# A hand-ordered attention stage with filler matmuls, row-packet loads and late expert weights

## The chip, the cores and the metric

One core of one Trainium2 chip. The metric is device time in microseconds (us) for one execution, median over runs.

## The reference, cut to what matters

```python
# attention: 8 batches x 8 heads, 576 positions, head size 64
q_p, k_p = phi(q), phi(k)        # relu(x)*cos | relu(x)*sin -> 128 features
kv  = einsum('bhsf,bhsd->bhfd', k_p, v);  z = sum(k_p, axis=2)
out = einsum('bhsf,bhfd->bhsd', q_p, kv) / (q_p . z + 1e-6)
# then 8 experts over 4608 tokens, routed by a balanced (Sinkhorn) table P
for e in range(8):
    out += P[:, e:e+1] * (relu(x @ w1[e]) @ w2[e])
```

## The kernel before: the parts that matter

The attention stage works on 32 head pairs, one after the other in the source; a scheduler orders the instructions on each engine.

```python
ps_num = tile_pool(name="ps_num", bufs=2, space=PSUM)   # also ps_kv 1, ps_tr 3, ps_x 2: 8 banks
for b in range(B):
    for hk in range(NPAIR):
        nc.sync.dma_start(out=q_ld[:, :, 0, :], in_=q_src)      # 256 B rows
        nc.scalar.copy(out=q_ld[:, :, 1, :], in_=q_ld[:, :, 0, :])
        nc.sync.dma_start(out=k_ld, in_=k[...].rearrange("(p c) d -> p c d", c=CH))  # 2304 B; v too
        if b == 0 and hk == 0: w_pre = load_expert_weights(0)
        # VectorE: v_aug (cast), k_p (two passes with cos and sin)
        for hh in range(2):
            # TensorE: nine matmuls of 64 rows into kv_ps[:, hh, :]
            nc.scalar.copy(out=kv_sb[:, hh, :], in_=kv_ps[:, hh, :])
        # TensorE: nine transposes of q into tr_ps; VectorE: ten q_pT
        for hh in range(2):
            # TensorE: five num matmuls; VectorE: five reciprocals (rden)
            # ScalarE: five divisions, st <- num_ps * rden
        # TensorE: five transposes of st into x_ps; VectorE or ScalarE copies x_ps to xT
...
# then logits, Sinkhorn, and 8 experts: 4608 matmuls of 512 columns
```

The softmax here doesn't subtract the row's maximum and nothing guards it: scores larger than these inputs give would overflow.

## Time and profile before

| | before |
|---|---|
| median of 4 runs | 1244.45 us (1244.02 to 1245.35) |
| span of the profiled run | 1240.2 us |
| first expert matmul | 226.3 us |
| time for one head pair, steady | 6.66 us |
| VectorE's own work for a pair | 4.75 us |

The prediction shows the lines that carry this. Two more, from the view of who waited for whom between 60 and 200 us (columns: total us, times, longest us), show the ping-pong of the two engines:

```profile
DVE rden L296 <- PE num_ps L285: 35.6, 40, 1.6
...
PE kv_ps L247 <- DVE k_p L232: 11.1, 20, 1.1
```

VectorE waits for TensorE's num, TensorE for VectorE's k features, and 32 pairs pay for both.

### The profile page before, as it was taken

To read this page: it belongs to the slowest core of one execution; us is meant where nothing else is said; L and a number is where in the kernel's file an instruction comes from. 1 tells how busy PE (TensorE), PEld (TensorE's weight loads), DVE (VectorE), ACT (ScalarE), POOL (GpSimd) and SP (SyncE) were. 2 spreads that over 40 slices of the span, in tenths; PEclk is the share of its full clock that TensorE was granted. 3 is DMA by queue.
4 is the path that set the end of the run, shared out by engine and by line. 5 is a ranking of instruction groups with operands and counts; after the bars stand their busy time and mean duration, and the time that the engine had idled before them with its cause. 6 is when DMAs were issued, how large, how long until landed. Compare 5 with 4: busy or idle time off the path is not lost.

```text
span 1240.2 us, 15100 instructions
## 1 busy us (share of the span) xinstructions
PE 1180.9 (95%) x6032; PEld 577.7 (47%) x6128; DVE 431.5 (35%) x1158; ACT 466.4 (38%) x1051; POOL 1.8 (0%) x10
## 2 busy tenths in 40 slices
PE   4888888899999999999999999999999999999997
PEld 3555555444444444444444444444444444444443
DVE  6776777563132213221322232223222322212221
ACT  4565554531333333333333333333333333333332
POOL 0000000000000000000000000000000000000000
PEclk9655555799999999999999999999999999999999
DMA  9856430300030003000300030003000100001122
GB/s 299 238 127 200 144 115 2 137 1 1 1 128 9 1 1 121 15 1 1 117 20 1 1 115 22 1 1 113 25 1 1 68 1 1 1 1 68 68 80 90
DMA packets 64743, 72.30 MB, mean 58 GB/s; under 512 B 39585, under 2 KB 39585, under 8 KB 64673
## 3 DMA queue, kind: packets, MB, share of 16 engines
q1 hardware_dynamic: 64672, 71.33, 17.7%
q8 instruction: 48, 0.79, 0.3%
q14 instruction: 23, 0.18, 0.0%
HBM read 61.88 MB, written 9.44 MB: 58 GB/s over the span
## 4 chain that ended last, share of the span: by engine, by line
PE 88%; DVE 7%; issue 2%; DMA 1%; ACT 1%; SPq 0%; DVEq 0%; ACTq 0%
PE y_ps L413 40%; PE h_ps L397 39%; PE tr_ps L262 4%; PE kv_ps L247 3%; PE num_ps L285 2%; DVE k_p L232 2%; DVE v_aug L227 1%; DMA wst<-in_moe_w_dram 1%; DVE rden L296 1%; DVE q_pT L270 0%; DVE colp L359 0%; ACT kv_sb L254 0%; PE x_ps L312 0%; ACT st L302 0%; PE lg_ps L333 0%
## 5 line engine op out<-in xcount | busy, mean ns | idle before, releaser
L404 ACT ACTIVATE hT<-h_ps 128x512 bf16<-128x512 f32 x576 | 343.9, 597 | 649.9 <-PE h_ps L397 627.5
L397 PE MATMUL h_ps<-xT,w1e 128*128 128x512 bf16 x2255 | 511.6, 380 | 2.8 <-issue 0.4
L413 PE MATMUL y_ps<-w2e,hT 128*128 128x512 bf16 x2257 | 506.2, 379 | 2.4
L430 DVE SCALAR_TENSOR_TENSOR out_acc<-y_ps,P_tok,out_acc 128x512 f32<-128x512 f32 x252 | 189.2, 751 | 620.3 <-PE y_ps L413 595.7
L413 PEld LDWEIGHTS <-hT 128*128 128x128 bf16 x2304 | 225.4, 98 | 271.0
L397 PEld LDWEIGHTS <-w1e 128*128 128x128 bf16 x2304 | 223.6, 98 | 266.6 <-issue 0.6
L262 PE MATMUL tr_ps<-ident_f,q_ld 128*128 128x128 f32 x288 | 86.9, 431 | 6.7 <-ACT q_ld L213 6.1
L302 ACT ACTIVATE st<-num_ps,rden 128x64 bf16<-128x64 f32 (+1 forms) x320 | 70.5, 314 | 40.1 <-DVE rden L296 37.4
L247 PE MATMUL kv_ps<-v_aug,k_p 64*128 64x65 bf16 x576 | 42.0, 235 | 32.1 <-DVE k_p L232 24.7
L270 DVE SCALAR_TENSOR_TENSOR q_pT<-tr_ps,cs2b 128x128 bf16<-128x128 f32 (+1 forms) x320 | 63.0, 261 | 0.2 <-PE tr_ps L262 0.2
L262 PEld LDWEIGHTS tr_ps<-ident_f,q_ld 128*128 128x128 f32 x288 | 47.2, 210 | 12.2 <-issue 6.0
L247 PEld LDWEIGHTS <-k_p 64*128 64x128 bf16 x576 | 31.5, 122 | 43.1 <-DVE k_p L232 28.9
L422 DVE TENSOR_SCALAR out_acc<-y_ps,P_tok 128x512 f32<-128x512 f32 x36 | 26.9, 750 | 60.0 <-PE y_ps L413 59.9
L285 PE MATMUL num_ps<-kv_sb,q_pT 128*128 128x65 bf16 (+1 forms) x320 | 47.5, 248 | 0.3 <-DVE q_pT L270 0.2
L232 DVE SCALAR_TENSOR_TENSOR k_p<-k_ld,cs 128x576 bf16<-128x576 f32 x64 | 45.2, 742 | 0.9 <-ACT cs L147 0.8
L296 DVE RECIPROCAL rden<-num_ps 128x1 f32<-128x1 f32 (+1 forms) x320 | 27.0, 151 | 51.0 <-PE num_ps L285 49.2
L285 PEld LDWEIGHTS <-q_pT 128*128 128x128 bf16 (+1 forms) x320 | 32.5, 132 | 18.4 <-issue 6.9
L312 PE MATMUL x_ps<-ident_bf,st 128*128 128x128 bf16 (+1 forms) x160 | 33.8, 275 | 5.6 <-ACT st L302 4.2
L254 ACT CAST kv_sb<-kv_ps 128x65 bf16<-128x65 f32 x64 | 13.9, 217 | 51.2 <-PE kv_ps L247 48.8
L108 DVE CAST w1e<-wst 128x2048 bf16<-128x2048 f32 x16 | 19.0, 1222 | 37.4 <-PE h_ps L397 36.9
L312 PEld LDWEIGHTS <-st 128*128 128x128 bf16 (+1 forms) x160 | 16.6, 105 | 29.7 <-ACT st L302 16.9
L213 ACT COPY q_ld<-q_ld 128x576 f32<-128x576 f32 x32 | 21.6, 674 | 9.5 <-DMA q_ld<-in_q_dram 9.4
(41 smaller groups left out, 118.3 us busy)
## 6 DMA issues: line engine op xcount, KB each, us to landing
wst<-in_moe_w_dram SPq DMA_DIRECT2D x32, 1024.0 KB, 6.3
q_ld<-in_q_dram SPq DMA_DIRECT2D x32, 288.0 KB, 3.7
k_ld<-in_k_dram SPq DMA_DIRECT2D x32, 288.0 KB, 4.0
v_ld<-in_v_dram SPq DMA_DIRECT2D x32, 288.0 KB, 4.2
out_dram<-out_acc SPq DMA_DIRECT2D x9, 1024.0 KB, 4.3
wg_ld<-in_moe_w_gate_dram SPq DMA_DIRECT2D x1, 16.0 KB, 2.0
```

Of the source, the lines that this page charges most:

```text
L232: nc.vector.scalar_tensor_tensor(out=k_p[:, :, a, :], in0=k_ld[:], scalar=0.0, in1=cs[:, :, a, :], op0=ALU.max, op1=ALU.mult,)
L247: nc.tensor.matmul(out=kv_ps[:, hh, :], lhsT=k_p[p0 : p0 + HP, c, :, :].rearrange("p a d -> p (a d)"), rhs=v_aug[p0 : p0 + HP, c, :], star ...
L262: nc.tensor.transpose(out=tr_ps[:, i, :], in_=q_ld[:, c, :, :].rearrange("p a d -> p (a d)"), identity=ident_f[:],)
L270: nc.vector.scalar_tensor_tensor(out=q_pT[:, hh, s0 : s0 + ln], in0=tr_ps[:, i, p0 : p0 + ln], scalar=0.0, in1=cs2b[:, s0 : s0 + ln], op0= ...
L285: nc.tensor.matmul(out=num_ps[:rows, si, :], lhsT=q_pT[:, hh, s0 : s0 + rows], rhs=kv_sb[:, hh, :], start=True, stop=True,)
L296: nc.vector.reciprocal(out=rden[:rows, si : si + 1], in_=num_ps[:rows, si, D : D + 1])
L302: nc.scalar.activation(out=st[:rows, si, hh * D : (hh + 1) * D], in_=num_ps[:rows, si, 0:D], func=AF.Copy, scale=rden[:rows, si : si + 1],)
L312: nc.tensor.transpose(out=x_ps[:, s0 : s0 + rows], in_=st[:rows, si, :], identity=ident_bf[:rows, :rows],)
L397: nc.tensor.matmul(out=h_ps[:, :ntok], lhsT=w1e[:, kt, ft * P : (ft + 1) * P], rhs=xT[:, kt, tj0 : tj0 + ntok], start=(kt == 0), stop=(kt ...
L404: nc.scalar.activation(out=hT[:, ft, :ntok], in_=h_ps[:, :ntok], func=AF.Relu)
L413: nc.tensor.matmul(out=y_ps[:srows, :], lhsT=hT[:, ft, ts0 : ts0 + srows], rhs=w2e[:, ft, :], start=(ft == 0), stop=(ft == FT - 1),)
L430: nc.vector.scalar_tensor_tensor(out=out_acc[:srows, cidx, :], in0=y_ps[:srows, :], scalar=P_tok[:srows, cidx, e : e + 1], in1=out_acc[:sr ...
```

## The change

Its intent: run the attention stage as a pipeline over pairs in a fixed order, and give TensorE enough to do that its clock is granted in full.

```diff
-            pattern=[[1, CH]], channel_multiplier=CH,
+            pattern=[[P, CH]], channel_multiplier=1,
...
-        ps_x = ... bufs=2
+        ps_fill = ... bufs=1
+        ps_x = ... bufs=1
...
-   in_=k[...].rearrange("(p c) d -> p c d", c=CH)      # v too
+   in_=k[...].rearrange("(c p) d -> p c d", p=P)
...
-   # kv: 2 x 9 matmuls of 64 rows
+   # kv: 2 x (4 matmuls of 128 rows and one of 64)
...
+        def fill(count=1):
+            for _ in range(count):
+                pn.tensor.matmul(out=fill_ps[:], lhsT=ident_bf[:], rhs=fill_src[:], ...)  # zeros, 512 columns
+        for n in range(5): load(n)
+        dup(0); stage_a(0); stage_kv(0); transposes(0, 0..2); dup(1)
+        for n in range(NP):
+            load(n + 5)
+            q_feature(n, 0..2)                   # VectorE
+            transposes(n + 1, 0); fill()         # TensorE
+            num(n, 0); fill(); num(n, 1); fill()
+            stage_a(n + 1)                       # VectorE: v_aug, k_p
+            transposes(n + 1, 1); transposes(n + 1, 2); fill()
+            dup(n + 2)                           # ScalarE
+            x_transpose(n - 1); fill()
+            stage_kv(n + 1); fill()              # TensorE, with the kv copies on ScalarE
+            divide(n, 0); divide(n, 1)           # VectorE rden, ScalarE st
+            x_copy(n - 1)
+            if n in (8, 12): w_issue(...) x2     # expert 0's weights
+            if n in (11, 15): w_cast(...) x2     # VectorE
```

Everything called through `pn` keeps this order on its engine. (`n` beyond the ends is guarded in the source.)

## The prediction

> **What bounds the kernel now.** I read the page first (busy shares, slices, chain), then the chain in order of time over the attention stage, then the timeline of a few head pairs, then windows of 1 us and of 0.25 us. The page says that TensorE is busy nearly throughout, and where its clock is low:
>
> ```profile
> PE 1180.9 (95%) x6032; PEld 577.7 (47%) x6128; DVE 431.5 (35%) x1158; ACT 466.4 (38%) x1051; POOL 1.8 (0%) x10
> PEclk9655555799999999999999999999999999999999
> ...
> PE 88%; DVE 7%; issue 2%; DMA 1%; ACT 1%; SPq 0%; DVEq 0%; ACTq 0%
> ```
>
> A slice is 31 us. So slices 2 to 7 are the attention stage (32 head pairs) at half clock. The first expert matmul starts at 226.4 us in the timeline; from there the expert stage lasts some 1014 us at full clock and the change does not touch it. Only the first 226 us can move. The chain in order of time shows one pair of that stage:
>
> ```profile
> 130.28 0.65 DVE v_aug L227
> 130.98 0.56 issue
> 131.54 0.76 DVE k_p L232
> 132.34 0.69 PE kv_ps L247 x9
> 133.32 0.65 PE kv_ps L247 x9
> 134.50 0.83 PE tr_ps L262 x3
> 136.94 0.65 DVE v_aug L227
> ```
>
> v_aug comes back after 6.66 us: that is the pace. The chain alternates: VectorE makes the k features, TensorE multiplies, VectorE waits again. In 60 to 200 us the reciprocals waited 35.6 us for num_ps, kv_ps waited 11.1 us for k_p. No engine is full; it is a ping-pong at half clock. VectorE's own work for a pair is read from starts:
>
> ```profile
> 129.86 0.42 DVE L296 RECIPROCAL rden<-num_ps 128x1 f32<-128x1 f32 x5 [1.09 <-PE num_ps L285]
> 130.21 0.73 DVE L227 CAST v_aug<-v_ld 128x576 bf16<-128x576 f32 x1
> 130.88 0.74 DVE L232 SCALAR_TENSOR_TENSOR k_p<-k_ld,cs 128x576 bf16<-128x576 f32 x1
> 131.54 0.75 DVE L232 SCALAR_TENSOR_TENSOR k_p<-k_ld,cs 128x576 bf16<-128x576 f32 x1
> 132.21 1.93 DVE L270 SCALAR_TENSOR_TENSOR q_pT<-tr_ps,cs2b 128x128 bf16<-128x128 f32 x10
> ```
>
> Start to start: 0.35 for five reciprocals (twice), 0.67 three times, about 1.87 for q_pT, and half an x copy (0.36/2): 4.75 us. That is VectorE's floor.
>
> **What the clock does to TensorE.** The first row below is at half clock, the others ran while it was full:
>
> ```profile
> 24.27 0.67 PE L247 MATMUL kv_ps<-v_aug,k_p 64*128 64x65 bf16 x9 [6.22 <-DVE k_p L232]
> 30.38 0.44 PE L285 MATMUL num_ps<-kv_sb,q_pT 128*128 128x65 bf16 x5
> 30.76 0.88 PE L262 MATMUL tr_ps<-ident_f,q_ld 128*128 128x128 f32 x6
> 36.39 2.11 ACT L302 ACTIVATE st<-num_ps,rden 128x64 bf16<-128x64 f32 x10 [0.61 <-DVE rden L296]
> 39.75 0.44 PE L247 MATMUL kv_ps<-v_aug,k_p 64*128 64x65 bf16 x9 [0.31 <-ACT kv_sb L254]
> ```
>
> ```profile
> 40.00:41.00 1.00, 1.00 (x14) 0.79 (x11) 1.00 (x9) 0.45 (x2) 0.00 (x0) 0.62 1.20 305
> 41.00:42.00 1.00, 1.00 (x9) 0.88 (x8) 0.12 (x3) 0.76 (x4) 0.00 (x0) 0.50 1.16 283
> ```
>
> The column before DMA is the granted clock: full, then half from about 40.6 us, for the rest of the stage. It also reads full before 29.5 us, where the durations say half, so durations decide. The loss followed 3.4 us in which TensorE was busy about two thirds.
>
> **What the Trainium skill says.** "TensorE: Matmul & The Clock Gate", Part 1, has a binary clock, half by default, full after about 3.4 us of sustained activity, lost after a quiet window. The trace agrees on two levels and a loss, and adds that an interleaved stage busy 85% in half-clock time (25.4 of 30 us at 170 to 200 us) never regains it. Part 4 of that page says transposes do not count as busy. This trace neither proves nor refutes it: the clock rose at 29.5 us after 1.97 us of transposes, but matmuls ran too. "DMA: Bandwidth & Descriptors", section "Specifications", asks for at least 512 B a descriptor for full rate. The trace shows a milder cost, in windows with 256 B q packets (first two rows) and with 2304 B k and v packets (last):
>
> ```profile
> 125.25:125.50 0.25, 0.00 (x0) 0.00 (x0) 0.25 (x1) 0.14 (x1) 0.00 (x0) 0.50 0.73 170
> 125.50:125.75 0.25, 0.07 (x2) 0.08 (x3) 0.25 (x3) 0.00 (x0) 0.00 (x0) 0.50 0.83 193
> 127.25:127.50 0.25, 0.25 (x7) 0.25 (x6) 0.25 (x2) 0.16 (x2) 0.00 (x0) 0.50 0.87 313
> ```
>
> Rate over share: 233 GB/s against about 360.
>
> **The change, part by part.**
> 1. Layout: k and v go from nine rows on a partition to one row a packet. A pair's three loads become 3 x 0.295 MB / 233 GB/s = 3.8 us of DMA instead of some 2.9. Hidden as long as the pace is over 3.8, with five pairs loaded ahead. In exchange kv takes 10 matmuls for 18, most of 128 rows. That saves about 0.3 us of TensorE at half clock, less if a 128-row weight load is slower, as num suggests (0.07 us apart warm, kv 0.042).
> 2. Six fills a pair, 512 columns of zeros into a spare bank. The expert matmuls run 0.216 us apart, so a fill is 0.22 us at full clock, 0.43 at half: 1.3 or 2.6 us a pair. They are there for the clock.
> 3. The order is fixed and pipelined by one pair. VectorE: q(n), k/v features(n+1), reciprocals(n), x copy(n-1). ScalarE: q copy(n+2), kv copies(n+1), ten divisions(n). The half-row waits of the chain above go.
> 4. Expert 0's weights (4 MB) move out of the start, where wst waits held up the second pair's loads until 14.3 us and the chain to 21 us.
> 5. One x_ps buffer less pays for the fill bank.
>
> **What sets the new pace.** VectorE needs 4.75, ScalarE about 0.67 + 0.42 + 2.11 + 0.32 = 3.5, DMA 3.8, TensorE warm about 4. But the fixed order closes a loop over num_ps, which has two buffers: the divisions of n must free the second before num(n+1) writes it, and ScalarE has the kv copies of n+2 ahead of the divisions of n+1. Summed at full clock: ten divisions 2.11; hand-over 0.05; five num 0.38; fill 0.22; five transposes 0.55 (0.11 each); fill 0.22; five x transposes 0.40; fill 0.22; first half of kv 0.42, its copy 0.22, hand-over 0.05 (the second half waited for that copy before, 0.31 above); second half 0.42; copy 0.21. Sum 5.47, say 5.5 us against VectorE's 4.75, so this loop is the bound. The gain is 1.2 us a pair, not the 1.9 that VectorE would allow.
>
> **Does the clock hold?** Array time a pair: fills 1.28, transposes 0.96, x 0.24, num and kv 0.54, together 3.0 of 5.5 us, 55%. Before, windows that kept the clock held about 45 to 50% by the same count, and the one that lost it about 30%. At half clock TensorE would be busy over 90% of the loop, denser than anything that failed to regain it. So warm, with 88%.
>
> **The end of the stage.** The features need the cosine table: v0 lands near 7.8 us (1 us later than before, from part 1) and v_aug stands ahead of the angle on VectorE. Then two table passes to 10.1, the other half of cs2b and the q copy to 11.5, kv and nine cold transposes: q(0) starts at 13.4. The first pair runs mostly cold: divisions(0) start near 20. Thirty loops of 5.5 lead to 185 for divisions(30). The last pair without a successor takes 5.4 more: divisions(30) 2.1, a copy 0.6, ten divisions 2.1, the x transposes 0.5. Expert matmuls start at 190.4 instead of 226.4: 36 us. The first expert matmuls, half clock until about 231 before, may start warm: 1.5 us. 1244.45 - 37.5 = 1207 us.
>
> **The rivals.**
> - The clock stays at half. The same loop then is 2.11 + 0.05 + 0.5 + 3 x 0.43 + 1.15 + 0.7 + 0.95 + 0.85 = 7.6 us. Divisions(0) at 21, end near 255: about 1272. For it: busy shares of 85% did not help before. Against: the density above.
> - VectorE is the bound because the loop is shorter than I sum: 4.75 to 5.1 a pair, an end at 168 to 178, about 1185 to 1195.
> - DMA becomes the bound: 73,728 more packets less 8,192. At 3.8 us it has 1.7 us to spare; it would need 5.5. Even with the 11 us of weights spread over eight pairs it is under that. It would only show in the first pairs.
> - Transfers and waits taken off the start are partly given back: the single num chain of the last pair, and the late cs table, both counted above.
>
> **Range and chances.** An error of 0.5 us in the loop is 15 us of time. 1188 to 1230 holds a loop from 4.9 to 6.2 at full clock; the cold case lies outside. Faster by over 2% means below 1219.6, a loop under 5.9: 0.80. Same 0.13. Slower, nearly all of it the cold case: 0.07.
>
> **What would show it.** The slices: full clock from the second on. Divisions first to first of the next pair: 5.5 us, num_ps waiting for st for about 0.6 us in each pair, hardly any wait of VectorE on TensorE that matters. DMA share in the stage near 0.7. The first expert matmul at 185 to 195, the rest unchanged at some 1014 us. Wrong if the clock column stays at 0.5, if the pace is VectorE's with no idle time on it, or if the waits name k_ld or v_ld.

## The result

| | before | after |
|---|---|---|
| median | 1244.83 us (12 runs) | 1209.54 us (8 runs, 1207.73 to 1210.88) |
| ratio, 95% interval | | 0.9717 (0.9708 to 0.9727) |
| span of the profiled run | 1240.2 us | 1209.1 us |
| first expert matmul | 226.3 us | 196.0 us |
| from there to the end | 1013.9 us | 1013.1 us |
| steady pace of a pair | 6.66 us | 5.48 us |

A ratio is the mean time of one kernel's runs over that of the other's in the same rounds, so not quite the ratio of the medians quoted. The gain is in the attention stage: 30.3 of the 31.1 us between the two spans. The profiled run of before, at 1242.0 us, was a short one, and of a rare kind: of 30 further runs of that kernel whose mean granted clock is on record, 3 have the trace's mean of 0.922, and these took 1241.1 to 1242.6 us; the other 27 (mean 0.914, 0.999 or 1.0) took 1243.3 to 1245.8.

The page of the kernel after: the slices' clock, and the chain by engine.

```profile
PEclk9989999999999999999999999999999999999999
...
PE 88%; ACT 6%; DVE 4%; issue 1%; DMA 0%; SPq 0%
```

The clock is full but for a dip in the third slice. On the chain ScalarE (6%) has taken the place that VectorE (7% before, 4% now) had. One period of the timeline of the kernel after (start, duration, engine, what; in brackets the idle time before and what ended it) shows why:

```profile
100.06 2.11 ACT L215 ACTIVATE st<-num_ps,rden 128x64 bf16<-128x64 f32 x10
...
102.22 0.43 PE L215 MATMUL num_ps<-kv_sb,q_pT 128*128 128x65 bf16 x5 [0.25 <-ACT st L215]
...
102.81 0.71 PE L215 MATMUL tr_ps<-ident_f,q_ld 128*128 128x128 f32 x5
...
103.57 0.52 PE L215 MATMUL x_ps<-ident_bf,st 128*128 128x128 bf16 x5
...
104.25 0.42 PE L215 MATMUL kv_ps<-v_aug,k_p 128*128 128x65 bf16 x5
...
104.71 0.22 ACT L215 CAST kv_sb<-kv_ps 128x65 bf16<-128x65 f32 x1 [1.44 <-PE kv_ps L215]
104.98 0.42 PE L215 MATMUL kv_ps<-v_aug,k_p 64*128 64x65 bf16 x5 [0.30 <-ACT kv_sb L215]
...
105.54 2.11 ACT L215 ACTIVATE st<-num_ps,rden 128x64 bf16<-128x64 f32 x10
```

Read it as a ring: the ten divisions end, num may reuse its buffer, TensorE goes through its order to kv, ScalarE copies kv, and only then come the next divisions, 105.54 - 100.06 = 5.48 us later. VectorE is not in it.

What the prediction did not have stands in the chain in order of time, around two places with a pair of weight casts each. The first:

```profile
78.65 2.27 DVE w1e L215 x2
80.92 0.80 DVE q_pT L215 x4
81.76 1.11 PE tr_ps L215 x4
83.72 0.54 PE fill_ps L215
...
89.09 2.12 ACT st L215 x10
```

The divisions before this stretch start at 79.61, so this pair takes 9.48 us instead of 5.48; the one with w2e's casts takes 8.31 (105.54 to 113.85). Together 6.8 us. The casts hold back q_pT, TensorE stands idle for 2.09 us, and then its clock is half until about 88.3 us, as the window rows say (the column before DMA share is the granted clock). At the second place the gap is again 2.09 us, and the clock is half from about 108.7 to 112.2 us. The rows of the first:

```profile
80.00:82.00 2.00, 0.24 (x1) 0.24 (x2) 2.00 (x8) 2.00 (x10) 0.00 (x0) 0.86 0.79 168
82.00:84.00 2.00, 2.00 (x11) 1.28 (x11) 2.00 (x7) 0.28 (x1) 0.00 (x0) 0.50 0.83 227
...
88.00:90.00 2.00, 1.45 (x12) 0.90 (x13) 1.27 (x2) 1.24 (x7) 0.00 (x0) 0.94 1.25 268
```

### The profile page after: what moved, and what is told of

Read it like the earlier page. It is cut to its first block, busy times and chain, and to the rows that moved or that the text cites.

```text
span 1209.1 us, 14947 instructions
## 1 busy us (share of the span) xinstructions
PE 1148.0 (95%) x5945; PEld 553.3 (46%) x6064; DVE 428.5 (35%) x1159; ACT 457.9 (38%) x1050; POOL 1.8 (0%) x10
## 4 chain that ended last, share of the span: by engine, by line
PE 88%; ACT 6%; DVE 4%; issue 1%; DMA 0%; SPq 0%
PE y_ps L547 41%; PE h_ps L531 40%; ACT st L215 5%; PE fill_ps L215 2%; PE tr_ps L215 2%; PE num_ps L215 1%; PE kv_ps L215 1%; PE x_ps L215 1%; DVE q_pT L215 1%; DVE xT L215 1%; DVE colp L493 0%; ACT kv_sb L215 0%; DMA v_ld<-in_v_dram 0%; PE lg_ps L467 0%; DVE P_tok L486 0%
## 5 line engine op out<-in xcount | busy, mean ns | idle before, releaser
L215 ACT ACTIVATE st<-num_ps,rden 128x64 bf16<-128x64 f32 (+1 forms) x320 | 67.6, 321 | 0.0
L215 PE MATMUL fill_ps<-fill_src,ident_bf 128*128 128x512 bf16 x168 | 66.6, 400 | 0.0
L215 PE MATMUL tr_ps<-ident_f,q_ld 128*128 128x128 f32 x288 | 45.4, 289 | 4.6 <-DVE q_pT L215 4.2
L215 PE MATMUL num_ps<-kv_sb,q_pT 128*128 128x65 bf16 (+1 forms) x320 | 28.4, 201 | 22.6 <-ACT st L215 22.3
L215 PE MATMUL kv_ps<-v_aug,k_p 128*128 128x65 bf16 (+1 forms) x320 | 27.4, 197 | 20.4 <-DVE k_p L215 10.6
L215 PEld LDWEIGHTS <-q_pT 128*128 128x128 bf16 (+1 forms) x320 | 23.8, 101 | 41.9 <-issue 29.7
L215 PEld LDWEIGHTS tr_ps<-ident_f,q_ld 128*128 128x128 f32 x288 | 36.4, 149 | 10.5 <-DVE q_pT L215 4.8
L215 PEld LDWEIGHTS <-k_p 128*128 128x128 bf16 (+1 forms) x320 | 17.3, 98 | 33.4 <-issue 17.3
L215 DVE CAST v_aug<-v_ld 128x576 bf16<-128x576 f32 x32 | 23.6, 739 | 4.6 <-DMA v_ld<-in_v_dram 4.6
```

The source lines that it names most:

```text
L215: ins = fn(**kw)
```

## The experiments

Theory A, mine: the pace is the ring over num_ps at full clock; the fills hold the clock; the layout is hidden; the casts cost 6.8 us. Rivals: the order alone holds the clock (B); the clock alone is the gain and the order idle (C); VectorE is the bound (D); the start without weights is the gain (E). Twelve kernels ran, all with right results.

### No fills

```diff
-        def fill(count=1):
+        def fill(count=0):
```

> The changed kernel without its fills. My theory: the fills keep the clock. Without them the array streams 1.74 us a pair, about 32 to 36% of the time, near the 30% that lost the clock before, so most of the stage runs at half clock; the num_ps loop without its three fills is then 6.3 us a pair instead of 5.48, and the time about 1235 us (1225 to 1240). Rival: the fixed order alone is dense enough. Then the clock stays at full, the loop shrinks to about 4.85 us, and the time is about 1190 us.

Measured: 1225.87 us, ratio to before 0.985. The window row of 100 to 140 us of this kernel:

```profile
100.00:140.00 40.00, 31.74 (x217) 23.69 (x217) 33.27 (x161) 21.09 (x87) 0.00 (x0) 0.50 0.83 163
```

Half clock in all of it, with TensorE busy 79%. The divisions follow one another every 6.07 us, but for 7.5 us in the two pairs with casts. So the fills hold the clock (B falls), and what is left of the change, at half clock, is still worth 19 us. My 6.3 us a pair was too long by 0.2, hence 1226 and not 1235.

### The divisions ahead of the kv copies

```diff
-            if n + 1 < NP:
-                stage_kv(n + 1)
-            fill()
             divide(n, 0)
             divide(n, 1)
+            if n + 1 < NP:
+                stage_kv(n + 1)
+            fill()
```

> The changed kernel with the divisions of pair n put ahead of the kv copies of pair n+1, which changes the order of ScalarE alone. My theory: this opens the loop over num_ps, VectorE becomes the bound at 4.75 to 4.95 us a pair against 5.48, and the time falls by 16 to 22 us to about 1190 us; num_ps no longer waits for st. Rival 1: TensorE's own work with its fills is the bound, and the pace stays near 5.4 us (1205 to 1210). Rival 2: the kv multiplication now waits for the divisions, a new loop of the same length, and nothing changes.

Measured: 1208.48 us, no gain, a miss. num_ps no longer waits for st, as expected, but pairs now take 4.5 and 6.1 us in turn. Timeline of this kernel, across a long one:

```profile
130.60 2.10 ACT L215 ACTIVATE st<-num_ps,rden 128x64 bf16<-128x64 f32 x10 [0.48 <-PE num_ps L215]
...
131.97 0.46 DVE L215 COPY xT<-x_ps 128x576 bf16<-128x576 bf16 x1 [1.02 <-PE x_ps L215]
...
136.72 2.11 ACT L215 ACTIVATE st<-num_ps,rden 128x64 bf16<-128x64 f32 x10 [2.64 <-DVE rden L215]
...
138.98 0.42 PE L215 MATMUL kv_ps<-v_aug,k_p 64*128 64x65 bf16 x5 [1.96 <-ACT kv_sb L215]
```

VectorE waits 1.02 us in its fixed order for the x transpose before it may begin q_pT, the divisions wait for VectorE's reciprocals, and the second half of kv waits 1.96 us behind the divisions. Opening one ring closed another of nearly the same length (the second rival), and the clock was also half for stretches of 3.4 us in pairs without casts, which took 7.5 to 7.7 us (at 40, 64 and 170 us). This run therefore can't tell whether num_ps was the bound; the third num_ps buffer below can.

### The casts in halves

```diff
-            if n in (8, 12): w_issue(...) x2
-            if n in (11, 15): w_cast(...) x2        # 2.3 us of VectorE in one pair
+            if n in (8, 16): w_issue(...) x2
+            if 11 <= n < 15 or 19 <= n < 23: w_cast_half(...)   # 0.6 us in each of eight pairs
```

> The changed kernel with each of the four weight casts of expert 0 on VectorE cut in two halves of about 0.6 us, one half in a pair, instead of two whole casts (2.35 us) in each of two pairs. My theory: the two stretches at 78 to 89 and 104 to 114 us, where q_pT waits for the casts and the clock is lost, cost 6.9 us together and go; time about 1203 us, clock full through the stage. Rival: the stretches are a chance loss of the clock or a DMA burst, and the time stays at 1209 us.

Measured: 1202.92 us (1202.6 to 1203.27). In the profile the divisions stay 5.47 to 5.48 us apart from the first pair to the last but one. The clock is full where the changed kernel first lost it, and the fills there take 0.38 to 0.39 us, as at full clock:

```profile
74.00:84.00 10.00, 8.34 (x74) 5.50 (x75) 8.62 (x43) 6.30 (x26) 0.00 (x0) 1.00 1.10 221
84.00:94.00 10.00, 7.76 (x71) 5.16 (x72) 9.73 (x42) 6.51 (x27) 0.00 (x0) 1.00 1.06 207
```

VectorE had 5.48 - 4.75 = 0.73 us free in each pair and a half cast fits in. 6.6 us came back of the 6.8 that the two stretches cost. Chance falls as a rival: all eight runs of the changed kernel have a mean clock of 0.994 to 0.996, all four of this one 0.999 or 1.0. The run also moved the second load of weights from pair 12 to 16, so a burst of DMA is excluded for the first stretch alone, whose load stayed at pair 8.

### The old layout in the new order

```diff
-   in_=k[...].rearrange("(c p) d -> p c d", p=P)          # v too, and the iota
+   in_=k[...].rearrange("(p c) d -> p c d", c=CH)
-   # kv: 2 x 5 matmuls, one row a packet
+   # kv: 2 x 9 matmuls of 64 rows, nine rows on a partition
```

> The changed kernel with the old layout of k and v (nine rows on a partition, 2304 B packets, 18 matmuls of 64 rows for kv). My theory: the layout is hidden either way; DMA share falls by about a quarter, nine matmuls 0.042 us apart take the 0.38 us that five 0.07 us apart take now, the first pair starts up to 1 us earlier, and the time stays within 3 us of 1209 us. Rival: the full-height matmuls carry a part of the gain, and the time rises by 8 us or more.

Measured: 1215.17 us, 5.6 more than the changed kernel: outside my 3 us, short of the rival's 8. A lighter DMA did not help: between 60 and 75 us its share fell from 1.04 to 0.64, and nothing got faster. The pace rose to 5.63 us: a weight load that now waits 0.1 us behind the fill ahead of kv, and the two halves of kv, each 0.03 to 0.04 us longer. The ring has no slack, so 0.15 us x 30 is 4.5 of the 5.6 us. At full clock the layout is not hidden: that part of A falls.

### Fills in the old order

```diff
+   fill(v_aug[:, 0:8, 0:D])            # after each half of kv
+   fill(q_pT[:, hh, 0:512]) x2         # after each half of num; ps_x loses a buffer
```

> The kernel before with six fills a pair (512 columns of that pair's own data, so that they stay with the pair; one x_ps buffer less pays for their bank), its order otherwise left to the scheduler. My theory: fills alone bring the clock back, but the ping-pong between VectorE and TensorE stays, so the pace falls only to 5.7 to 6.4 us from 6.66, and the time lies at 1218 to 1238 us. Rival: the clock is nearly all of it, and the time is at 1215 us or below. Second rival: the idle gaps of the ping-pong still lose the clock, the fills run at half clock, and the time rises over 1250 us.

Measured: 1222.2 us; the k features come every 5.78 us between 42 and 146 us and the first expert matmul at 207.2. The granted clock is 0.84 to 1.00 in windows of 20 to 29 us between 60 and 200 us, so the fills bring most of it, not all. Fills alone are worth 22 us, the rest of the change without fills 19 (above), both 35: they overlap. That each shortens the other's waits is my reading, not shown. C falls as a full account.

### The weights late in the old order

```diff
-                if b == 0 and hk == 0:
+                if pair_idx == 8:
                     w_pre = load_expert_weights(0)
```

> The kernel before with the load of expert 0's weights moved from the first pair to the ninth, nothing else. My theory: the second pair's loads no longer stand behind the weights, the chain no longer waits on wst up to 21 us, and some 5 to 9 us are saved: 1236 to 1240 us. Rival: the pairs then wait for their own loads or for the casts later, and the time stays at 1244 us.

Measured: 1246.92 us, ratio 1.0019 (1.001 to 1.0027): slightly slower, a miss, and E falls. The k features of the second pair come some 6 us earlier, but those of the fifth begin at the same 37.5 in both kernels. In the trace of before, the work held up by the weights came in a rush, and the clock was full from about 30.0 to 40.2 us; here it never is, and the casts then put the k features back by 4.5 us between the eighth pair and the eleventh. Both things are in this kernel's trace, but its clock column does not show the first. How much the rush is worth stays open: in 23 of the 30 runs of before counted above the mean clock is 0.999 or 1.0, as in all 13 here, so they may have had no rush either. Window row and timeline:

```profile
24.00:60.00 36.00, 30.30 (x222) 20.02 (x223) 26.18 (x129) 18.90 (x72) 0.00 (x0) 1.00 0.59 181
```

```profile
32.38 0.67 PE L247 MATMUL kv_ps<-v_aug,k_p 64*128 64x65 bf16 x9 [0.52 <-DVE k_p L232]
33.35 0.65 PE L247 MATMUL kv_ps<-v_aug,k_p 64*128 64x65 bf16 x9 [0.30 <-ACT kv_sb L254]
```

The column says 1.00, and the run's mean clock is given as 0.999. Nine kv matmuls at full clock take 0.44 to 0.46 us; here they take 0.65 to 0.67, the durations of half clock. In these traces the column reads full until a first change is recorded. Durations decide.

### The layout alone in the old order

```diff
-   in_=k[...].rearrange("(p c) d -> p c d", c=CH)         # v too, and the iota
+   in_=k[...].rearrange("(c p) d -> p c d", p=P)
-   # 2 x 9 kv matmuls
+   # 2 x 5 kv matmuls
```

> The kernel before with the new layout of k and v and the 10 kv matmuls alone. My theory: undoing it in the changed kernel cost 0.15 us a pair, so alone it is worth no more than that at half clock either: the time lies within 5 us of 1244 us, the clock stays at half and the DMA share rises by a third. Rival: the full-height matmuls are dense enough to bring the clock back, and the time falls by more than 10 us.

Measured: 1238.79 us, ratio 0.9953: 5.3 us faster, just past my 5. The clock is half for most of the stage, but full in six stretches of 3.4 us between 75 and 181 us (0.57 in the window from 100 to 150 us), where before it was half throughout. Pairs at half clock take 6.35 and 6.51 us in turn, those touched by full clock 5.98 to 6.25. From one half of kv to the next it is now 0.85 us (five matmuls in 0.54 and a copy) where it was 0.98, twice a pair. That is 0.26 us, enough for the 0.23 by which the half-clock pace fell. So the second rival holds in a small part; how the 5.3 us divide is not shown.

### The fills moved, then a third num_ps buffer

The fills are written into the tr_ps tile that the transposes then overwrite; their bank is free. The first run keeps two num_ps buffers as a control, the second takes the bank.

```diff
             tr_ps = ps_tr.tile([P, TB, P], FP32, ...)
+            # two fills into tr_ps (n > 0)
-        ps_fill = ... bufs=1
-        ps_num = ... bufs=2
+        ps_num = ... bufs=3          # second run only
```

> Control for the next run: the changed kernel with its six fills moved into the tr_ps tiles just ahead of the transposes, which frees their bank; num_ps keeps two buffers. My theory: four fills now lie in the num_ps loop instead of three, so the pace is 5.5 to 5.75 us and the time 1208 to 1217 us; num_ps still waits for st in each pair.

> The same with the freed bank given to num_ps, three buffers. My theory: the loop over num_ps now holds five divisions instead of ten, 4.5 to 4.7 us, and VectorE becomes the bound at 4.75 to 4.95 us a pair; against the control the time falls by 20 to 28 us to about 1188 us (1182 to 1195), and num_ps waits little for st. Rival: something else (the order of x copies on VectorE, as after the divisions were put first, or TensorE itself) holds the pace at 5.3 us or more, and the time stays over 1203 us.

Measured: 1223.32 and 1193.71 us. The control's pace is 5.70 us, inside the estimate, but its time is above it: the fills now wait with the transposes for q_pT (7.1 us in all between 60 and 175 us), and the clock is lost for longer (pairs of 9.9, 7.1, 8.8 and 7.1 us around the casts and one of 7.2 at the start). That the waits lose the clock is argued. With the third buffer the divisions come 4.70 and 4.90 us apart in turn. Timeline of that kernel, VectorE in one of the longer pairs:

```profile
129.12 0.46 DVE L214 COPY xT<-x_ps 128x576 bf16<-128x576 bf16 x1
...
129.49 1.93 DVE L214 SCALAR_TENSOR_TENSOR q_pT<-tr_ps,cs2b 128x128 bf16<-128x128 f32 x10
...
133.34 0.74 DVE L214 RECIPROCAL rden<-num_ps 128x1 f32<-128x1 f32 x10
...
134.01 1.91 DVE L214 SCALAR_TENSOR_TENSOR q_pT<-tr_ps,cs2b 128x128 bf16<-128x128 f32 x10
```

No bracket names a wait: in this longer pair VectorE is the bound, at the 4.75 to 4.95 us expected of it. (The shorter pairs have no x copy on VectorE; the last run below shows what holds them at 4.70.) So num_ps was the bound in the control, and by the same ring with one fill less (5.70 - 0.22 = 5.48) in the changed kernel: D falls there. 29.6 us of time hung on one PSUM buffer against the control.

### From there to a kernel that beats both

```diff
 # e10: third num_ps buffer and the casts in halves
 # e11: also all x copies on ScalarE
 # e12: also the casts on ScalarE, in quarters over sixteen pairs
```

> Three num_ps buffers (as in the run before) and the weight casts in halves over eight pairs. In that run the two pairs with whole casts took 9.9 us against 4.8, 10.3 us lost in all. My theory: VectorE is the bound, so the 4.9 us of casts stay on the path but the lost clock does not: 5 to 6 us faster, 1186 to 1190 us. Rival: if the loss were only the idle gap and not VectorE's time, all 10 us come back: 1183 us or below.

> The same with all x copies on ScalarE. My theory: VectorE's work falls from 4.80 to about 4.55 us a pair, but the loop through five divisions lies at 4.6 to 4.7, so the pace falls by 0.1 to 0.2 us: 3 to 6 us faster than the run with split casts. Rival: ScalarE's longer copies (0.65 us) delay the kv copies and the time stays or rises.

> The same with the casts also on ScalarE, in quarters over sixteen pairs. My theory: ScalarE has about 0.7 us free a pair, a quarter takes about 0.6 us, so most of the 4.9 us of casts disappears: 3 to 5 us faster than the run before it. Rival: the quarters stand ahead of the kv copies on ScalarE and stretch the loop, no gain.

Measured: 1188.92, 1184.61 and 1182.85 us (ratios to before 0.9554, 0.9518, 0.9505). The first gained 4.8 us; its eight pairs with half casts still take 5.1 to 5.5 us, as VectorE, now the bound, does the casts. The second brings 4.3 us: 4.70 us a pair, now without the 4.90. The third brings 1.8 and not 3 to 5: in the second the pairs with casts were only some 1.0 us over 4.70 in all, so most of the casts already fitted on VectorE. In this last kernel every pair takes 4.69 to 4.70 us, and num_ps waits for st again in each pair, 0.2 us at most (view of waits, 60 to 150 us):

```profile
PE num_ps L214 <- ACT st L214: 3.1, 19, 0.2
```

The ring is back with five divisions in it: the control's 5.70 less 1.0 for five divisions is 4.70. The last kernel is 26.7 us faster than the change.

## Why the prediction was right

**The bound and its size: right.** Each term of the ring against one period of the trace, us:

| term | predicted | measured |
|---|---|---|
| ten divisions, hand-over | 2.16 | 2.16 |
| five num, fill | 0.60 | 0.59 |
| five transposes, fill | 0.77 | 0.76 |
| five x transposes, fill | 0.62 | 0.68 |
| first half of kv, copy, hand-over | 0.69 | 0.73 |
| second half of kv, last copy | 0.63 | 0.56 |
| sum | 5.47 | 5.48 |

That the ring, not something of equal length, set it is shown by the third buffer: the same order and fills at 4.80 instead of 5.70.

**The clock: right.** Full in the slices, regained during the first pair (fills from 16.8 us on take 0.39, those before 0.61 and more). Without fills it is half. That zeros of no use to anyone bring the clock is measured; how dense the work must be is not: TensorE busy 79% (no fills) and 85% (before, 170 to 200 us) of the time at half clock did not bring it. (The prediction's 29.5 and 40.6 us for the short full clock of before are a little off: the kv matmuls at 29.99 are the first with full-clock durations, and 0.62 in the window from 40 to 41 us puts the drop at 40.24.)

**VectorE, DMA and the start: right in kind.** VectorE stayed off the bound, k_ld and v_ld name no wait after the first pair, and the first divisions began at 19.3 (predicted 20). The DMA term was too small: the prediction took 233 GB/s of full share from windows of 0.25 us and expected a share near 0.7. With 256 B rows in all three loads the windows of 10 us from 24 to 54 us moved 211 to 219 GB/s at a share of 1.07 to 1.33, only 165 to 205 of full share. It did no harm, and the last kernel moved 218 to 224 GB/s at a share of 1.11 to 1.16 without a wait for a load, so a share of 1 is not a ceiling. The guess that the taken-off start is partly given back was even too mild: moved alone, it gave nothing.

**The layout: right in the prediction, wrong in my later expectations.** "Hidden as long as the pace is over 3.8" holds for the loads. For the kv matmuls the prediction said about 0.3 us a pair at half clock; 0.26 was measured there, and 0.15 at full clock. The expectations of the two layout runs had at most 0.15 and nothing for these. Its reading of the matmuls' spacing was wrong, though: 0.07 us for num with 128 rows of weights against 0.042 for kv with 64 is a mean over unlike steps. In the single records of the trace, matmuls start 0.03 to 0.04 us apart with 64 rows and with 128; one step of about 0.12 us comes where the size of the weights changes (102.31 to 102.43 for the last num, 104.35 to 104.47 for the last kv of a half).

**The term that was missing: the casts.** The prediction moves expert 0's weights and lists their DMA time, but not their place on VectorE. Two casts in a row are 2.3 us where a pair has 0.73 to spare, and after the gap that they open in TensorE the clock is half for a while: 6.8 us, of which splitting them gave back 6.6. The stage therefore ended at 196.0, not at 190.4: 190.4 + 6.8, less 0.7 for the start and 0.6 for thirty rings of 5.48, gives 195.9.

**Why the total still fits.** 196.0 instead of 190.4 would put the time near 1213. The expert stage came out 0.8 us shorter, where 1.5 was allowed: 0.7 more (its first matmuls did not start warm: the clock was half from 194.1 to 197.5 us). Against it, the profiled run of before was 2.5 us shorter than the median that I subtracted from (1241.98 against 1244.45), so the 226.4 us from which I counted was a short stage; the profiled run after was 1.3 us long. The hit at 1209.5 is a right mechanism plus a missed loss that these differences between runs partly cover; that they did so is luck.

## What to carry to other kernels

In a fixed order, write down the ring through each buffer that is reused (last reader, next writer, whatever the order puts between) and compare its length with the busiest engine: here one more PSUM buffer was worth 15.8 us against the changed kernel, and the rest of the tuning 10.9. Place every side job, such as a cast, by the slack of the pair that it falls into, because here a gap of 2 us on TensorE cost its own length and, at both places, the clock as well. Judge the clock by the durations of a known instruction, not by the column alone.

## What the Trainium skill lacked or had wrong

- "TensorE: Matmul & The Clock Gate", section "Why this matters for your kernels", allows idle gaps of up to about 3 us between bursts. In the changed kernel an idle gap of 2.09 us was followed by half clock until about 88.3 us (transposes at 81.8 take 1.11 us for four, against 0.60 to 0.65). Not every such gap was: with the divisions ahead, after one of 2.06 us up to 84.45 the fills still took 0.38 to 0.39 us until 87.9.
- The same page, Part 1: it tells of two clock levels and unreliable events, but not that the profile's clock reads full before the first change. In the run with late weights it reads 1.00 (mean 0.999) where nine kv matmuls take the 0.65 to 0.67 us of half clock.
- Part 4 of the same page says that transposes do not count towards the clock. No run here decides it.
- No page has the effect that useless matmuls pay: 16 us of the 35 (1225.87 against 1209.54 us).
